# Neighbouring steps and the order of weight conversions in the first pair of an attention and two-FFN kernel

## The chip, the core and the metric

The program runs on one NeuronCore of a Trainium2 chip. Five engines have queues of their own, and each works through its queue in the order in which the program was written: TensorE (PE, with the weight loads shown apart as PEld), VectorE (DVE), ScalarE (ACT), GpSimd (POOL) and SyncE (SP), which here only issues DMAs. An instruction that has to wait for another engine holds up everything behind it in its own queue. The metric is the device time of one execution in microseconds; lower is better.

## What is computed

Attention over the feature axis, and two feed-forward networks one after the other, on 6016 tokens of width 256 with a hidden width of 2048:

```python
qn = q / (norm(q, axis=1) + 1e-06); kn = k / (norm(k, axis=1) + 1e-06)
a = softmax(kn.T @ qn / tau)              # 256 x 256
x = v @ a                                  # 6016 x 256
h = x @ w_in;  g = h * clip(h + 3, 0, 6) / 6;  x = g @ w_out     # first FFN
h = x @ w_in2; g = max(h, 0) ** 2;             out = g @ w_out2  # second FFN
```

The result has to be good to fp32. PE multiplies in the fast fp32r format, so every operand is kept as a high part and a rest, and each product is three matmuls: high x high, rest x high, high x rest. The high part is a cast on ACT (`nc.scalar.copy` in `split`, L124 of the profile), the rest is a subtraction on DVE or POOL (L126).

## The kernel before

The tokens are cut into six *pairs* of two blocks (n = 0 and 1, up to 512 tokens each). The attention matrix is folded into the first layer: v @ a @ w_in is computed as v @ (a @ w_in), so the first-layer weights of the first FFN are products too, called *m1* in the code, made in four quarters c4 (tiles `mp` in PSUM, then `wa_<c4>h` and `wa_<c4>l`, and `a` for a part of them). From the second pair on, eight products are done as seven by Strassen's scheme, and all work stands in a list of events with a place each (`at`, `extra`, `run`).

The first pair is different, and it is what the change touches. Its weights are not ready when it begins. It runs 32 *steps*; step a is one block n and one slice f of 128 hidden features (from step 4 on a = 2f + n). In a step, in the words used below:

- **h(a)**, the first product on PE (`product`, `whole_product`; six matmuls at L311, the first ones at L321 to L323), into one of four PSUM banks taken in turn;
- **relu(a)** on ACT (L651; tile `r`) and **gate(a)** on DVE (L653; tile `g`), which reads the PSUM bank and `r` and frees the bank;
- **hi(a)** on ACT and **lo(a)** on DVE, the high part and the rest of g (tile `gs`, four buffers);
- **s(a)**, the second product on PE (`second_both`; six matmuls at L676, four that use hi(a), then two that use lo(a)), accumulated in `acc`.

`drain(LAG)` with LAG = 2 puts s(a-2) into step a, behind h(a+1).

Into the same queues go the conversions of the weights of the first FFN from float64 words, fourteen in this list: `wi1` (an eighth of w_in) and `wo1` (an eighth of w_out). A conversion has five stages: 0 `magnitude` (ACT, L155), 1 `sign` (ACT L158 and DVE L159), 2 `high` (DVE L162), 3 `low` (DVE L167), 4 the split (ACT L124, DVE L126). `START` gives each one its place: `issue()` is called twice in a step and each call does what the plan has for the next place. The last stage also calls `feed()`, which issues the DMA of a later unit on SP, into one of three staging slots. For the first five conversions (DENSE) the stages have five places in a row, for the others the places 0, 3, 4, 5 and 6 from the start.

A quarter of m1 is made in steps 5, 13 and 21 (`m1_whole`, two products into two PSUM banks), and taken out of PSUM one step later (`m1_out`: three casts on ACT at L493 and three rests on DVE at L495; `m1_keep`: two copies at L503). The first h that uses it is h(8), h(16) or h(24). POOL makes the sums and rests of the quarters 0 and 1 that the Strassen pairs need (`m`, L216, and the rests `wa_0l`, `wa_1l` at L126), and the operands of the second pair, at places of the event list that `run` reaches at the end of each step.

Of the kernel before, what the change touches and what calls it, by code (L numbers as in the profile page):

```python
# [12 lines left out]
AF = mybir.ActivationFunctionType  # L13
ALU = mybir.AluOpType
# [7 lines left out]
KC = C // P  # L22
# [8 lines left out]
LAG = 2  # L31
# [5 lines left out]
EARLY_AT = {15: (0, 1), 16: (2,), 18: (3, 4)}  # L37


START = [-5, -3, 0, 3, 6] + [9 + 4 * k for k in range(9)]  # L40
DENSE = 5
SIGN = -(2 ** 31)
APART = 2.6
# [13 lines left out]
def attention_then_two_ffns(  # L57
# [30 lines left out]
    nc = tc.nc  # L88
# [25 lines left out]
    three = const.tile([P, 1], F32, name="three")  # L114
# [6 lines left out]
    def split(hi, lo, x, part=2, eng=nc.vector):  # L121

        if part != 1:
            nc.scalar.copy(hi, x)  # L124
        if part != 0:
            eng.tensor_tensor(out=lo, in0=x, in1=f32(hi), op=ALU.subtract)  # L126
# [46 lines left out]
    wi1, wo1 = {}, {}  # L173
# [151 lines left out]
    with tc.manual_schedule():  # L325
# [10 lines left out]
        for gi, n in enumerate(GROUPS):  # L336
            src = wpool.tile([P, 1024], F32, tag=f"wo{gi % NU}", name=f"qk{gi}")[:, :2 * n * C]
            nc.sync.dma_start(
                out=src.rearrange("p (t x c) -> p t x c", t=n, x=2), in_=qk[:, t:t + n, :, :]
# [5 lines left out]
            if gi == TAU_AT:  # L345
# [4 lines left out]
                    out=tq[:, 2:4], in0=tq[:, 2:4], scalar1=tau_sb, scalar2=1.0, op0=ALU.mult, op1=ALU.mult  # L350
# [11 lines left out]
        et = [hpool.tile([P, KC, C], F32R, tag="o", bufs=4, name=f"et{s}") for s in ("h", "l")]  # L362

        order = [
            ("wo1", 0), ("wi1", 2), ("wo1", 1), ("wi1", 3), ("wo1", 2), ("wi1", 4), ("wo1", 3), ("wi1", 5),
            ("wo1", 4), ("wi1", 6), ("wo1", 5), ("wi1", 7), ("wo1", 6), ("wo1", 7),
        ]
        loaded = []

# [100 lines left out]
        def m1_whole(c4, i):  # L470
            mps[c4, i] = bank([P, 512], f"mp{c4}_{i}")
            low_last(mps[c4, i], [
                ([t[:, j, :] for t in wi1[c4]], [t[:, i, j * P:(j + 1) * P] for t in et]) for j in range(KC)
            ], False)
# [138 lines left out]
        def tmp(tag, w, name, **kw):  # L613
            return hpool.tile([P, WMAX], F32, tag=tag, name=name, **kw)[:, :w]

        def g_tile(w, name):
            t = gpool.tile([P, 2, WMAX], F32R, tag="g", name=name)[:, :, :w]
            return [t[:, i, :] for i in range(2)]


        w0 = WIDTHS[0]
        steps = [(n, f) for f in range(KF) for n in range(2)]
        steps[:4] = [(0, 0), (0, 1), (1, 0), (1, 1)]
        hs = {}
        pending = []
# [8 lines left out]
        def product(at, k):  # L634
            if at < len(steps):
                n, f = steps[at]
                if k == 0:
                    hs[at] = bank([P, WMAX], f"h0_{n}_{f}")[:, :w0]
                passes(hs[at], [(weight0(f, k), x0[k, n])], k == 0, k == KC - 1)

        def whole_product(at):
            if at < len(steps):
                n, f = steps[at]
                hs[at] = bank([P, WMAX], f"h0_{n}_{f}")[:, :w0]
                low_last(hs[at], [(weight0(f, k), x0[k, n]) for k in range(KC)])

        def first(at_step, between):
            n, f = steps[at_step]
            h = hs.pop(at_step)
            r = tmp("r", w0, f"r0_{n}_{f}")  # L650
            nc.scalar.activation(r, h, AF.Relu, bias=three)  # L651
            g = tmp("g32", w0, f"g0_{n}_{f}")
            nc.vector.scalar_tensor_tensor(out=g, in0=r, scalar=6.0, in1=h, op0=ALU.min, op1=ALU.mult)  # L653
            between()
            gs = g_tile(w0, f"gs0_{n}_{f}")
            if at_step == len(steps) - 1:
                at(1.6, lambda: split(*gs, g, 0))
                at(3.0, lambda: split(*gs, g, 1))
            else:
                split(*gs, g)  # L660
            return gs

        def second(n, f, gs):
            return [
# [16 lines left out]
        def drain(limit):  # L681
            while len(pending) > limit:
                second_both(*pending.pop(0))


        plan = {}
        for k, at in enumerate(START):
            for st, after in enumerate(range(5) if k < DENSE else (0, 3, 4, 5, 6)):
# [4 lines left out]
        def issue():  # L693
            for k, st in sorted(plan.get(place[0], ())):
                loaded[k][st]()
                if st == 4:
                    feed()
            place[0] += 1
# [4 lines left out]
        def at(place, go):  # L703
            events.append((place, len(events), go))
# [158 lines left out]
        k = 0  # L863
# [67 lines left out]
        for kk in range(KC):  # L931
            for a in range(2):
                product(a, kk)
        for a, (n, f) in enumerate(steps):
            gs = first(a, issue)
            pending.append((n, f, gs))

            part, since = divmod(a + M1_LEAD, 8)
            if 0 < part < 4 and since == 1:
                for i in range(KC):  # L940
                    m1_out(part, i)
                m1_keep(part)
            late_products = (a + 1) % 8 == 0 and a < 24
            if late_products:
                drain(LAG)
            if a:
                whole_product(a + 1)
            if 0 < part < 4 and since == 0:
                for i in range(KC):
                    m1_whole(part, i)  # L950
            drain(LAG)
            issue()

            run(-(len(steps) - 1 - a) * SLOTS / 4)


        for x, go in zip(LEFT_AT, [(n, f, d, gs) for n, f, gs in pending for d in range(KC)], strict=True):
            n, f, d, gs = go
# [48 lines left out]
```

## Time and profile before

| what | value |
|---|---|
| median of 3 runs | 1042.24 us (1042.06 to 1043.7) |
| the profiled execution's own time | 1042.34 us |
| its span, first to last instruction | 1040.6 us |
| PE busy | 1031.6 us, 99% of the span |
| DVE busy | 852.5 us, 82% |
| ACT busy | 665.0 us, 64% |
| POOL busy | 28.9 us, 3% |
| PE clock granted | 1.00 of full speed (2.4 GHz) |
| share of the chain that ended last | PE 90%, DVE 3%, ACT 3%, DMA 2% |

A matmul's duration in the profile is longer than its distance to the next, since matmuls overlap; a PE that loses time can therefore look busy. What it loses is seen from the distance of its starts, or where the profile writes an idle time in brackets. In the timeline a line is a start in microseconds from the span's start, a duration in microseconds, engine, line, operation, written tile and read tiles, shapes, and the number of instructions merged into it; in brackets stands idle time just before it, and what ended it.

### The profile page before, as it was taken

How to read it: one execution, taken by the hardware profiler on the slowest of the kernel's cores; microseconds unless marked ns; L12 is line 12 of the kernel's file. 1: busy time of each engine (PE TensorE's matmuls, PEld its weight loads, DVE VectorE, ACT ScalarE, POOL GpSimd, SP SyncE). 2: the span in 40 equal slices, each digit the busy share in tenths (PEclk: the TensorE clock that was granted, in tenths of full speed). 3: DMA queues.
4: the chain of work that ended last, by engine and by line, in shares of the span. 5: the costliest groups of instructions: out<-in, count | busy, mean ns of one | idle time of the engine just before them, and what ended most of it. 6: DMA issues, size and time to landing. Idle time of an engine off the chain costs nothing.

```text
span 1040.6 us, 12968 instructions
## 1 busy us (share of the span) xinstructions
PE 1031.6 (99%) x4630; PEld 866.4 (83%) x4630; DVE 852.5 (82%) x1429; ACT 665.0 (64%) x1200; POOL 28.9 (3%) x33
## 2 busy tenths in 40 slices
PE   9999999999999999999999999999999999999998
PEld 8878788888888888888998888888888888888997
DVE  7898868889989889988988688688688688778765
ACT  6787777787788778877876445445445455445443
POOL 0012240000000000000000000000000000000000
PEclk9999999999999999999999999999999999999999
DMA  9911204003403403212755002002001100200100
GB/s 368 349 41 43 79 3 140 1 1 117 157 1 116 157 1 117 97 56 96 254 197 187 1 1 81 1 1 80 2 1 45 37 1 3 74 1 1 41 1 36
DMA packets 25936, 77.64 MB, mean 75 GB/s; under 512 B 2832, under 2 KB 4880, under 8 KB 25872
## 3 DMA queue, kind: packets, MB, share of 16 engines
q1 hardware_dynamic: 25872, 76.82, 20.9%
q8 instruction: 36, 0.59, 0.2%
q14 instruction: 28, 0.23, 0.1%
HBM read 52.95 MB, written 23.86 MB: 74 GB/s over the span
## 4 chain that ended last, share of the span: by engine, by line
PE 90%; DVE 3%; ACT 3%; DMA 2%; issue 1%; POOL 0%; ACTq 0%; SPq 0%; POOLq 0%
PE acc L323 15%; PE acc L321 15%; PE acc L322 15%; PE y L322 8%; PE y L321 8%; PE y L323 8%; PE q L321 4%; PE q L322 4%; PE q L323 4%; PE acc L676 2%; PE h L311 2%; PE x L321 2%; PE x L323 2%; PE x L322 2%; DMA qk<-in_qk 2%
## 5 line engine op out<-in xcount | busy, mean ns | idle before, releaser
L126 DVE TENSOR_TENSOR gs<-g,gs 128x512 fp32r<-128x512 f32 (+1 forms) x384 | 260.7, 679 | 59.8 <-ACT gs L828 47.8
L323 PE MATMUL acc<-gs,wo 128*128 128x512 f32 (+1 forms) x708 | 272.5, 385 | 0.1
L322 PE MATMUL acc<-gs,wo 128*128 128x512 f32 (+1 forms) x708 | 272.5, 385 | 0.0
L321 PE MATMUL acc<-gs,wo 128*128 128x512 f32 (+1 forms) x708 | 272.4, 385 | 0.0
L828 ACT CAST gs<-g 128x512 fp32r<-128x512 f32 (+1 forms) x352 | 208.1, 613 | 27.7 <-DVE g L819 19.0
L323 PEld LDWEIGHTS acc<-gs,wo 128*128 128x128 f32 x708 | 132.9, 188 | 25.3 <-DVE gs L126 0.5
L321 PEld LDWEIGHTS acc<-gs,wo 128*128 128x128 f32 x708 | 132.9, 188 | 24.4
L322 PEld LDWEIGHTS acc<-gs,wo 128*128 128x128 f32 x708 | 132.9, 188 | 24.3
L801 ACT COPY se<-y 128x512 f32<-128x512 f32 (+1 forms) x88 | 50.8, 577 | 124.0 <-PE y L323 123.9
L805 DVE TENSOR_TENSOR h<-q,se 128x512 f32<-128x512 f32 (+1 forms) x88 | 59.6, 678 | 65.6 <-ACT se L801 65.1
L801 ACT COPY su<-y 128x512 f32<-128x512 f32 (+1 forms) x88 | 50.9, 578 | 87.0 <-PE y L323 76.1
L824 DVE SCALAR_TENSOR_TENSOR g<-h 128x512 f32<-128x512 f32 (+1 forms) x144 | 97.0, 674 | 0.0
L811 ACT ACTIVATE r<-h,three 128x512 f32<-128x512 f32 (+1 forms) x120 | 85.5, 713 | 7.9 <-DVE h L805 7.7
L819 DVE SCALAR_TENSOR_TENSOR g<-r,h 128x512 f32<-128x512 f32 (+1 forms) x120 | 80.9, 674 | 3.9 <-ACT r L811 3.8
L813 ACT ACTIVATE r<-y 128x512 f32<-128x512 f32 (+1 forms) x48 | 28.3, 589 | 62.3 <-PE y L323 62.3
L805 DVE TENSOR_TENSOR h<-q,su 128x512 f32<-128x512 f32 (+1 forms) x88 | 59.5, 676 | 1.6
L805 DVE TENSOR_TENSOR h<-x,sa 128x512 f32<-128x512 f32 (+1 forms) x88 | 59.2, 673 | 0.0
L801 ACT COPY sa<-y 128x512 f32<-128x512 f32 (+1 forms) x88 | 50.8, 577 | 6.6 <-PE y L323 0.4
L824 DVE SCALAR_TENSOR_TENSOR g<-y,r 128x512 f32<-128x512 f32 (+1 forms) x48 | 32.7, 681 | 23.2 <-ACT r L813 22.7
L676 PE MATMUL acc<-gs,wo 128*128 128x512 f32 x180 | 45.5, 391 | 1.0 <-ACT gs L124 1.0
L300 PE MATMUL s<-qk 128*128 128x256 f32 x188 | 42.0, 385 | 0.0
L676 PEld LDWEIGHTS acc<-gs,wo 128*128 128x128 f32 x180 | 33.5, 188 | 9.1 <-ACT gs L124 2.2
(247 smaller groups left out, 1801.1 us busy)
## 6 DMA issues: line engine op xcount, KB each, us to landing
qk<-in_qk SPq DMA_DIRECT2D x23, 512.0 KB, 7.4
wo<-in_w_out SPq DMA_DIRECT2D x16, 512.0 KB, 5.1
wi<-in_w_in SPq DMA_DIRECT2D x10, 512.0 KB, 4.6
x2d<-o SPq DMA_DIRECT2D x20, 256.0 KB, 2.4
raw<-x2d SPq DMA_DIRECT2D x10, 512.0 KB, 5.8
out<-o SPq DMA_DIRECT2D x20, 256.0 KB, 2.2
raw<-in_vt SPq DMA_DIRECT2D x8, 512.0 KB, 5.9
wo2d<-wo2s SPq DMA_DIRECT2D x8, 512.0 KB, 2.9
```

What stands on the lines that cost most here:

```text
L126: eng.tensor_tensor(out=lo, in0=x, in1=f32(hi), op=ALU.subtract)
L300: nc.tensor.matmul(s_ps[i], lhsT=x[:, C + i * P:C + (i + 1) * P], rhs=x[:, :C], start=(t == 0), stop=(t == NT - 1))
L321: nc.tensor.matmul(ps, lhsT=ah, rhs=bh, start=first, stop=False, skip_group_check=more)
L322: nc.tensor.matmul(ps, lhsT=al, rhs=bh, start=False, stop=False, skip_group_check=more)
L323: nc.tensor.matmul(ps, lhsT=ah, rhs=bl, start=False, stop=last, skip_group_check=more)
L676: nc.tensor.matmul(acc[0, 0, n, d], lhsT=wo1[u][:, i, at + d * P:at + (d + 1) * P], rhs=gs[k], start=f == 0 and (i, k) == (0, 0), stop=f = ...
L801: nc.scalar.copy(s[tag], s["y"])
L805: nc.vector.tensor_tensor(out=s[which], in0=s[ps], in1=s[tag], op=ALU.add)
L811: nc.scalar.activation(s["r" + which], h, AF.Relu, bias=three)
L819: nc.vector.scalar_tensor_tensor(out=g, in0=s["r" + which], scalar=6.0, in1=h, op0=ALU.min, op1=ALU.mult)
L824: nc.vector.scalar_tensor_tensor(out=g, in0=h, scalar=0.0, in1=r, op0=ALU.max, op1=ALU.mult)
L828: nc.scalar.copy(gs[which][0], s["g" + which])
```

## The change

Two things are changed, both in the first pair. The function `first` is split into `relu0`, `gate0` and `part0`, and the loop calls them for different steps: in step a stand the relu of step a+1, the gate and the high part of step a, and the rest of step a-1. In the steps 7, 15 and 23 (`late_products`) s(a-2) goes ahead of h(a+1) as before, and relu(a+1) behind hi(a). Of the two m1 products the second goes behind the second product of the step. And in the table of conversions wi1 5 goes ahead of wo1 3, wi1 7 ahead of wo1 5, and all from the fifth on start at other places (the fifth at 10 where it was 6, the last at 46 where it was 41).

```diff
-START = [-5, -3, 0, 3, 6] + [9 + 4 * k for k in range(9)]
+START = [-5, -3, 0, 3, 10, 13, 17, 20, 25, 29, 33, 36, 41, 46]
...
-            ("wo1", 0), ("wi1", 2), ("wo1", 1), ("wi1", 3), ("wo1", 2), ("wi1", 4), ("wo1", 3), ("wi1", 5),
+            ("wo1", 0), ("wi1", 2), ("wo1", 1), ("wi1", 3), ("wo1", 2), ("wi1", 4), ("wi1", 5), ("wo1", 3),
...
-        def first(at_step, between):
...
-            nc.scalar.activation(r, h, AF.Relu, bias=three)
...
-            between()
-            gs = g_tile(w0, f"gs0_{n}_{f}")
...
-                split(*gs, g)
+        def relu0(at_step):
...
+                nc.scalar.activation(rs[at_step], hs[at_step], AF.Relu, bias=three)
+
+        def gate0(at_step):
...
+        def part0(at_step, part):
+            if at_step >= 0:
+                (hi, lo), g = gs0.pop(at_step) if part else gs0[at_step]
+                split(hi, lo, g, part)
...
+        relu0(0)
         for a, (n, f) in enumerate(steps):
-            gs = first(a, issue)
-            pending.append((n, f, gs))
-
             part, since = divmod(a + M1_LEAD, 8)
+            late_products = (a + 1) % 8 == 0 and a < 24
+            if late_products:
+                drain(LAG - 1)
+            if a:
+                whole_product(a + 1)
+            if not late_products:
+                relu0(a + 1)
+            pending.append((n, f, gate0(a)))
+            issue()
...
+                part0(a, 0)
+            if late_products:
+                relu0(a + 1)
+            part0(a - 1, 1)
             if 0 < part < 4 and since == 1:
                 for i in range(KC):
                     m1_out(part, i)
                 m1_keep(part)
-            late_products = (a + 1) % 8 == 0 and a < 24
-            if late_products:
-                drain(LAG)
-            if a:
-                whole_product(a + 1)
-            if 0 < part < 4 and since == 0:
-                for i in range(KC):
-                    m1_whole(part, i)
+            m1 = 0 < part < 4 and since == 0
+            if m1:
+                m1_whole(part, 0)
             drain(LAG)
+            if m1:
+                m1_whole(part, 1)
             issue()
```

What this does to the queues is shown at three places. The first is DVE at the start of the pair. In the names `g_0_0` is the g of block 0, slice 0 (step 0), `g_0_1` that of step 1, `gs_0_0` the rest of step 0; `tawi_2`, `tawo_1` are weights in conversion. Before:

```order
L653 SCALAR_TENSOR_TENSOR g_0_0_588<-r_0_0_586,h_0_0_572 128x512
L167 ISA tawi_2_536<-tawi_2_536,tywi_2_538 128x1024
L126 TENSOR_TENSOR gs_0_0_595<-g_0_0_588,gs_0_0_595 128x512
L126 TENSOR_TENSOR wi1l_599<-tawi_2_536,wi1h_598 128x512
L159 TENSOR_SCALAR tawo_1_591<-wo_1_432 128x512
L653 SCALAR_TENSOR_TENSOR g_0_1_608<-r_0_1_606,h_0_1_576 128x512
L162 SCALAR_TENSOR_TENSOR tawo_1_591<-tbwo_1_592,tawo_1_591 128x512
L126 TENSOR_TENSOR gs_0_1_611<-g_0_1_608,gs_0_1_611 128x512
```

and after the change, on the same engine and from the same instruction on:

```order
L658 SCALAR_TENSOR_TENSOR g_0_0_590<-r_0_0_586,h_0_0_572 128x512
L167 ISA tawi_2_536<-tawi_2_536,tywi_2_538 128x1024
L126 TENSOR_TENSOR wi1l_600<-tawi_2_536,wi1h_599 128x512
L159 TENSOR_SCALAR tawo_1_594<-wo_1_432 128x512
L658 SCALAR_TENSOR_TENSOR g_0_1_616<-r_0_1_588,h_0_1_576 128x512
L162 SCALAR_TENSOR_TENSOR tawo_1_594<-tbwo_1_595,tawo_1_594 128x512
L126 TENSOR_TENSOR gs_0_0_592<-g_0_0_590,gs_0_0_592 128x512
```

The rest of step 0, `gs_0_0`, which stood second behind its gate, now stands sixth, behind the gate of step 1.

The second place is ACT in step 6, where the first-layer weights `wa_1h` of quarter 1 are taken out of PSUM. The steps 5, 6 and 7 are `1_2`, `0_3` and `1_3` here. Before:

```order
L124 CAST gs_1_2_722<-g_1_2_716 128x512
L651 ACTIVATE r_0_3_754<-h_0_3_725,three 128x512
L158 ACTIVATE tywi_4_712<-raw13h 128x512
L124 CAST gs_0_3_760<-g_0_3_756 128x512
L493 ACTIVATE wa_1h<-mp_0_732,rs_504 128x2x128
```

and after:

```order
L124 CAST gs_1_2_713<-g_1_2_711 128x512
L158 ACTIVATE tywo_2_716<-wo_2_603 128x512
L653 ACTIVATE r_1_3_751<-h_1_3_744,three 128x512
L124 CAST gs_0_3_755<-g_0_3_753 128x512
L493 ACTIVATE wa_1h<-mp_0_720,rs_504 128x2x128
```

Ahead of the weights now stands the relu of step 7, `r_1_3`, where that of step 6 stood.

The third place is DVE around steps 9 (`1_4`), 10 (`0_5`) and 11 (`1_5`). Before:

```order
L653 SCALAR_TENSOR_TENSOR g_0_5_881<-r_0_5_879,h_0_5_859 128x512
L159 TENSOR_SCALAR tawi_5_845<-raw13l 128x512
L126 TENSOR_TENSOR gs_0_5_885<-g_0_5_881,gs_0_5_885 128x512
L162 SCALAR_TENSOR_TENSOR tawi_5_845<-tbwi_5_846,tawi_5_845 128x512
L653 SCALAR_TENSOR_TENSOR g_1_5_909<-r_1_5_907,h_1_5_888 128x512
L167 ISA tawi_5_845<-tawi_5_845,tywi_5_847 128x1024
L126 TENSOR_TENSOR gs_1_5_912<-g_1_5_909,gs_1_5_912 128x512
```

and after:

```order
L658 SCALAR_TENSOR_TENSOR g_0_5_876<-r_0_5_845,h_0_5_838 128x512
L159 TENSOR_SCALAR tawi_5_832<-raw13l 128x512
L126 TENSOR_TENSOR gs_1_4_849<-g_1_4_847,gs_1_4_849 128x512
L162 SCALAR_TENSOR_TENSOR tawi_5_832<-tbwi_5_833,tawi_5_832 128x512
L658 SCALAR_TENSOR_TENSOR g_1_5_904<-r_1_5_874,h_1_5_867 128x512
L167 ISA tawi_5_832<-tawi_5_832,tywi_5_834 128x1024
L126 TENSOR_TENSOR gs_0_5_878<-g_0_5_876,gs_0_5_878 128x512
```

The kinds of instruction and the conversion among them are the same; the two rests belong to one step earlier each.

## Rows read from the trace of the kernel before

**Rows 1.** Chain of waits, last steps of the first pair: start, us, what.
```profile
139.16 1.36 PE acc L676 x6
```

**Rows 2.** Timeline of PE, first pair: start us, us, what, idle before.
```profile
58.59 1.07 PE L311 MATMUL h<-x,wa_0h 128*128 128x512 f32 x4
...
61.31 1.52 PE L676 MATMUL acc<-gs,wo 128*128 128x512 f32 x6
...
72.20 0.50 PE L311 MATMUL mp<-wi1h,eth 128*128 128x512 f32 x1 [0.63 <-DVE g L653]
...
79.14 1.07 PE L311 MATMUL h<-x,wa_1h 128*128 128x512 f32 x4
...
119.16 1.65 PE L676 MATMUL acc<-gs,wo 128*128 128x512 f32 x6 [0.96 <-ACT gs L124]
...
152.59 0.39 PE L321 MATMUL y<-x,wa_0h 128*128 128x512 f32 x1
```

**Rows 3.** Waits from 50 to 157 us: us in total, times, longest.
```profile
DVE gs L126 <- ACT gs L124: 8.9, 16, 1.3
DVE g L653 <- ACT r L651: 8.1, 11, 1.3
```

**Rows 4.** Timeline of DVE, steps 0 and 1.
```profile
59.50 1.18 DVE L167 CUSTOM_DVE_ANT_0 tawi<-tawi,tywi 128x1024 uint16<-128x1024 uint16 x1
60.60 1.23 DVE L126 TENSOR_TENSOR gs<-g,gs 128x512 fp32r<-128x512 f32 x1
61.76 0.68 DVE L126 TENSOR_TENSOR wi1l<-tawi,wi1h 128x512 fp32r<-128x512 f32 x1
62.36 0.41 DVE L159 TENSOR_SCALAR tawo<-wo 128x512 int32<-128x512 int32 x1
62.69 0.67 DVE L653 SCALAR_TENSOR_TENSOR g<-r,h 128x512 f32<-128x512 f32 x1
63.29 0.68 DVE L162 SCALAR_TENSOR_TENSOR tawo<-tbwo,tawo 128x512 int32<-128x512 int32 x1
```

**Rows 5.** Timeline of ACT, step 0.
```profile
60.71 0.62 ACT L124 CAST wi1h<-tawi 128x512 fp32r<-128x512 f32 x1 [0.48 <-DVE tawi L167]
```

**Rows 6.** Timeline of ACT, around the m1 casts of step 6.
```profile
75.29 0.68 ACT L651 ACTIVATE r<-h,three 128x512 f32<-128x512 f32 x1
...
77.27 0.47 ACT L493 ACTIVATE wa_1h<-mp,rs 128x256 fp32r<-128x256 f32 x1
...
78.00 0.69 ACT L493 ACTIVATE wa_1h<-mp,rs 128x512 fp32r<-128x512 f32 x1
```

**Rows 7.** Timeline of POOL.
```profile
89.78 1.29 POOL L126 TENSOR_TENSOR wa_0l<-m,wa_0h 128x512 fp32r<-128x512 f32 x1 [1.80 <-ACT wa_0h L124]
...
92.04 1.07 POOL L216 TENSOR_TENSOR m<-m,m 128x256 f32<-128x256 f32 x1
...
94.22 1.24 POOL L216 TENSOR_TENSOR m<-m,m 128x256 f32<-128x256 f32 x1
...
112.30 2.58 POOL L126 TENSOR_TENSOR wa_1l<-m,wa_1h 128x512 fp32r<-128x512 f32 x2 [16.84 <-ACT wa_1h L124]
```

**Rows 8.** Timeline of DVE beside POOL's work from 89.78 on.
```profile
90.92 0.43 DVE L159 TENSOR_SCALAR tawi<-raw13l 128x512 int32<-128x512 int32 x1
91.70 0.81 DVE L126 TENSOR_TENSOR gs<-g,gs 128x512 fp32r<-128x512 f32 x1 [0.34 <-ACT gs L124]
92.43 1.23 DVE L162 SCALAR_TENSOR_TENSOR tawi<-tbwi,tawi 128x512 int32<-128x512 int32 x1
93.58 0.67 DVE L653 SCALAR_TENSOR_TENSOR g<-r,h 128x512 f32<-128x512 f32 x1
94.18 0.68 DVE L167 CUSTOM_DVE_ANT_0 tawi<-tawi,tywi 128x1024 uint16<-128x1024 uint16 x1
94.94 1.06 DVE L126 TENSOR_TENSOR gs<-g,gs 128x512 fp32r<-128x512 f32 x1
```

**Rows 9.** Timeline of DVE beside POOL's wa_1l.
```profile
113.97 1.46 DVE L167 CUSTOM_DVE_ANT_0 tawo<-tawo,tywo 128x1024 uint16<-128x1024 uint16 x1
```

More of the change, by code (lines that the diff above doesn't have):

```diff
@@ L364, in attention_then_two_ffns @@
         order = [
[L365 to L366 removed]
+            ("wo1", 0), ("wi1", 2), ("wo1", 1), ("wi1", 3), ("wo1", 2), ("wi1", 4), ("wi1", 5), ("wo1", 3),
+            ("wo1", 4), ("wi1", 6), ("wi1", 7), ("wo1", 5), ("wo1", 6), ("wo1", 7),
         ]
@@ L645, in whole_product @@
                 low_last(hs[at], [(weight0(f, k), x0[k, n]) for k in range(KC)])
-        def first(at_step, between):
+        rs, gs0 = {}, {}
+        def relu0(at_step):
+            if at_step < len(steps):
+                n, f = steps[at_step]
+                rs[at_step] = tmp("r", w0, f"r0_{n}_{f}")
+                nc.scalar.activation(rs[at_step], hs[at_step], AF.Relu, bias=three)
+        def gate0(at_step):
             n, f = steps[at_step]
-            h = hs.pop(at_step)
-            r = tmp("r", w0, f"r0_{n}_{f}")
-            nc.scalar.activation(r, h, AF.Relu, bias=three)
             g = tmp("g32", w0, f"g0_{n}_{f}")
-            nc.vector.scalar_tensor_tensor(out=g, in0=r, scalar=6.0, in1=h, op0=ALU.min, op1=ALU.mult)
-            between()
-            gs = g_tile(w0, f"gs0_{n}_{f}")
[L656 to L659, printed above, removed]
-                split(*gs, g)
-            return gs
+            nc.vector.scalar_tensor_tensor(
+                out=g, in0=rs.pop(at_step), scalar=6.0, in1=hs.pop(at_step), op0=ALU.min, op1=ALU.mult
+            )
+            gs0[at_step] = g_tile(w0, f"gs0_{n}_{f}"), g
+            return gs0[at_step][0]
+        def part0(at_step, part):
+            if at_step >= 0:
+                (hi, lo), g = gs0.pop(at_step) if part else gs0[at_step]
+                split(hi, lo, g, part)
         def second(n, f, gs):
@@ L933, in attention_then_two_ffns @@
                 product(a, kk)
+        relu0(0)
         for a, (n, f) in enumerate(steps):
-            gs = first(a, issue)
-            pending.append((n, f, gs))
             part, since = divmod(a + M1_LEAD, 8)
+            late_products = (a + 1) % 8 == 0 and a < 24
[7 more added lines that the diff above has]
+            issue()
+            if a == len(steps) - 1:
+                at(1.6, lambda: part0(len(steps) - 1, 0))
+                at(3.0, lambda: part0(len(steps) - 1, 1))
+            else:
+                part0(a, 0)
+            if late_products:
+                relu0(a + 1)
+            part0(a - 1, 1)
             if 0 < part < 4 and since == 1:
```

## Prediction

> **What bounds the kernel now.** I read the page first, then the chain of waits, then TensorE's (PE's) timeline of the first pair, then the other queues around its gaps. In the chain a block of six matmuls takes 1.36 us [rows 1], so one takes 0.2267 us while nothing holds PE. The change touches only the first pair, where PE runs its steps from 58.59 to 152.59 us [rows 2]. In between stand 396 matmuls: 30 products of 6, three pairs of m1 products (36), 30 second products of 6. They need 396 x 0.2267 = 89.77 us; the stretch takes 94.00. So 4.2 us are lost there, which is all that this change can win. Two of the gaps are seen directly [rows 2]: the second m1 product at 72.20 waited for its PSUM bank, which a gate of VectorE (DVE) still read, and the second product at 119.16 waited for a high part. After 152.59 PE is fed without gaps until the last evictions.
>
> I call h(a) the product of step a, relu(a) and hi(a) ScalarE's (ACT's) two instructions for it, gate(a) and lo(a) DVE's two, s(a) the second product, which uses hi(a) in its first four matmuls and lo(a) in its last two.
>
> **The change part by part.** No instruction is added or removed. Three things move: relu(a+1) goes ahead of gate(a) and hi(a); lo(a) goes from step a to step a+1, behind gate(a+1); the conversions start later and in another order. The sum is made against the profiled execution's 1042.34 us (1040.6 span and 1.7 around it), 0.1 us over the median of the runs, 1042.24.
>
> *Waits inside a step.* DVE loses 8.1 us waiting for a relu and 8.9 for a high part in this stretch [rows 3]. Both waits nearly go: relu(a) is a step old when gate(a) comes, hi(a) is done when lo(a) comes. That is worth something to PE only where DVE was late; it buys back the 4.2 us at most. What is late next is lo itself: it now has one step (12 matmuls, 2.72 us) less until s(a) needs it.
>
> *The first step: 2.0 us lost.* s(0) starts at 61.31 [rows 2], so its lo matmuls are due at 61.31 + 4 x 0.2267 = 62.22. Before, lo(0) stands at 60.60 and ends at 61.83 [rows 4], in time. After, DVE's queue from the L167 of the weights at 59.50 on is: rest of the weights, L159, gate(1), L162, lo(0). The L167 ends at 60.68, the cast of the weights on ACT runs from 60.71 to 61.33 as before [rows 4, 5], and the rest can start at 61.35 instead of 61.76. From there the starts follow at the distances of rows 4: L159 0.60 later (61.95), gate(1) 0.33 later (62.28), L162 0.60 later (62.88), lo(0) 0.60 later (63.48), and with the 0.68 of an undisturbed rest [rows 4] it ends at 64.16. PE waits 64.2 - 62.2 = 2.0 us. The same count one step on puts lo(1) at 67.1, with its matmuls due at 66.9: 0.2 more. From lo(2) on the rest is in time, since s(0)'s wait has moved all of PE back. Its bound from below would be 0, if DVE took the rows in another order; from above 2.5, with 0.1 for each restart.
>
> *The m1 bank and the high parts: those gaps go.* In step 5 the second m1 product now stands behind s(3), and gate(4), whose bank it takes, is done at 70.8 by the same count, before PE wants it. The other old gaps go with the old order, so of the 4.2 none is counted in the new kernel.
>
> *New first weights: 0, with 0.3 for each of three from above.* In step 6 relu(7) now stands on ACT ahead of hi(6) and of the three casts that make the first-layer weights of the next quarter. It waits for h(7). With 84 matmuls from 58.59 and the 2.2 us above, h(8), the first user of those weights, starts at 77.63 + 2.2 = 79.83 (before: 79.14 [rows 2]). h(7) ends three blocks earlier, at 77.2 with its tail; relu 0.68, a cast 0.62, two of 0.37 and one of 0.69 [rows 5, 6] end at 79.96. The first of them is there by 79.0, the last is due two matmuls into h(8), at 80.28. So it is just hidden. If that cover goes, PE waits at h(8), h(16) and h(24). What it does cost is DVE: lo(5) ends about 74.8 and the rests of these weights stand ahead of all else until ACT delivers, near 78.9: four idle microseconds, after which DVE's backlog has to be worked off at some 2.3 us of work per 2.72 us step (gate and lo 1.2, half a conversion of 0.33 + 3 x 0.60).
>
> *Steps 9 and 10: 1.2 us lost.* GpSimd (POOL) works from 89.78 to 95.46 [rows 7], and DVE's instructions with both operands in SBUF that begin inside a POOL instruction end only some 0.55 us after it: the L162 at 92.43 takes 1.23 us and ends at 93.66, POOL's ended at 93.11. The gate at 93.58, which reads PSUM, takes its 0.67 [rows 7, 8]. From 80.5, where the last rest of the new weights leaves DVE, thirteen instructions (12 x 0.60 + 0.33 = 7.5 us) and 1.7 us of waits (0.6 for casts, 1.1 behind POOL's first wa_0l) lead to the L159 at 89.8. From an L159 to the end of the second lo behind it DVE took 90.92 to 96.00 before [rows 8], 5.1 us. After, the same kinds begin 0.6 us before POOL's second wa_0l is through, so lo(9) ends at 89.8 + 0.6 + 1.6 = 92.0 and lo(10) at 89.8 + 0.6 + 5.1 = 95.5. Counting 60 matmuls from h(8), s(9)'s lo is due at 91.6 and s(10)'s at 94.3. PE waits 0.4, then 95.5 - 94.7 = 0.8. Before, the second lo of that row was lo(11), needed much later. Bounds: 0, if POOL misses these instructions (six of them undisturbed take 3.3 us: lo(10) at 93.1), and 1.9.
>
> The Trainium skill ("SBUF — State Buffer", section "Who interferes with whom") says that a VectorE instruction with two SBUF inputs fully blocks against a GpSimd instruction that reads SBUF, and one with a single SBUF input does not. By that rule every lo and every L162 and L167 can be held and no gate, which leaves both of these terms as they stand; a reader who took the two as sharing bandwidth would put them near 0 and get 1041.0. The rows agree with the rule.
>
> *Step 18: 1.7 us lost.* The same with wa_1l: POOL's two run 2.58 us without a gap [rows 7], and the L167 that met them took 1.46 [rows 9]. After, the two casts that release them stand two instructions behind hi(16) on ACT, while DVE comes to L162, gate(17), L167 and lo(16). Walking both queues on from h(16) with the same distances, POOL starts 1.95 us before lo(16) is due; the L167 is held by the first, lo(16) by the second, and lo(16) ends 2.58 + 0.55 + 0.55 = 3.7 us after POOL's start: 1.7 late. Bounds 0 and 1.8.
>
> *Start table and DMAs: 0.* Each weight is still finished before its first use (wo_3, now behind two wi units, ends a step ahead of s(12)). The second pair's load now stands on SP behind wo_6, which waits for a staging slot, some 5 us later than before; POOL's two sums from it fall into steps 21 and 22, where DVE is waiting anyway, and the second pair starts ten steps later. If that cover goes, up to 0.8 is lost at 152.59. It goes into the upper end.
>
> *Sum.* New gaps 2.2 + 1.2 + 1.7 + 0.7 for restarts and the third quarter = 5.8, against 4.2 before: +1.6, so **1043.9 us**. With all bounds low 2.6 - 4.2 = -1.6 (1040.7), with all high 2.5 + 0.9 + 1.9 + 1.8 + 0.8 = 7.9, +3.7 (1046.0).
>
> **The rivals.**
> *The port collisions miss.* ACT's casts set when POOL runs, and half a microsecond of drift is enough. Then only the start and the restarts remain, 2.6 us: 1040.7. For it: the old kernel met the same POOL work and lost little. Against it: the two meetings are set by neighbouring rows, not by chance.
> *Faster for good.* The freed 17 us of DVE waits are real at the start too: DVE reaches lo(0) by 62.2, the new order loses under 1 us in all: 1042.3 - 3.4 = 1038.9. It decides whether the L159, gate(1) and L162 delay lo(0). Against it: the four stand in front of it in the queue.
> *Slower: relu(a+1) blocks ACT.* At each of the three m1 steps relu waits for a product behind 18 other matmuls while the casts that need nothing stand behind it. If DVE's backlog then reaches PE again after each, at 1 us each beside the collisions, the sum is +3.5: 1045.8. It decides from the point where the casts end after 80.3. Against it: the count above ends at 79.96.
>
> **How the numbers follow.** About 0.2% (2.1 us: 1040.2 to 1044.3) is what a measurement can tell here. Forecast 0.50, own range 1042.6 to 1045.2, of which 0.29 lies under 1044.3 and 0.21 over it. Collisions miss 0.20, nearly all within 0.2%. Faster 0.15. Slower 0.15. So faster 0.17, same 0.47, slower 0.36. The range 1039.8 to 1045.8 leaves out most of the faster case and the top of the slower.
>
> **What would show it.** A gap on PE of about 2 us at s(0), put down to DVE's gs; none before the second m1 product of step 5; DVE idle for some 4 us ahead of the wa_1l rests; PE held by gs of DVE near 92 to 96 and near 115; h(8) near 79.8 and the second pair's first product near 154. The forecast is wrong if s(0) runs through, or if PE loses under 3 us between 58.6 and that product.

## The result, and the profile after

The changed kernel takes 1050.05 us (median of 6 runs, 1048.49 to 1051.74), the kernel before beside it 1042.15 us. The ratio is 1.0074, 95% interval 1.0063 to 1.0084: slower by 7.9 us. 1043.9 had been forecast, with 1045.8 as the upper end. The profiled execution took 1048.49 us with a span of 1046.7 us, 6.1 us over the span before. The 1.5 us between it and the median are taken up under the clock below. The forecast misses the median by 6.1 us: 5.0 are lost in the stretch shown next beyond the 5.8 that were forecast, 1.5 are these, and 0.5 come back because the stretch began earlier.

All of it is in the first pair. This is the timeline of PE in that stretch, columns as in [rows 2]:

```profile
58.12 1.07 PE L311 MATMUL h<-x,wa_0h 128*128 128x512 f32 x4
...
60.84 1.07 PE L682 MATMUL acc<-gs,wo 128*128 128x512 f32 x4
63.80 0.73 PE L682 MATMUL acc<-gs,wo 128*128 128x512 f32 x2 [1.89 <-DVE gs L126]
...
79.59 1.07 PE L311 MATMUL h<-x,wa_1h 128*128 128x512 f32 x4
...
83.81 0.73 PE L682 MATMUL acc<-gs,wo 128*128 128x512 f32 x2 [0.33 <-DVE gs L126]
...
95.74 0.73 PE L682 MATMUL acc<-gs,wo 128*128 128x512 f32 x2 [0.47 <-DVE gs L126]
...
105.84 1.39 PE L311 MATMUL h<-x,wa_2h 128*128 128x512 f32 x4
107.07 0.92 PE L311 MATMUL h<-x,wa_2l 128*128 128x512 f32 x2
...
117.11 0.74 PE L682 MATMUL acc<-gs,wo 128*128 128x512 f32 x2 [1.38 <-DVE gs L126]
...
120.85 0.73 PE L682 MATMUL acc<-gs,wo 128*128 128x512 f32 x2 [0.69 <-DVE gs L126]
...
138.83 0.74 PE L682 MATMUL acc<-gs,wo 128*128 128x512 f32 x2 [0.71 <-DVE gs L126]
...
148.56 0.74 PE L682 MATMUL acc<-gs,wo 128*128 128x512 f32 x2 [1.24 <-DVE gs L126]
...
158.71 0.39 PE L321 MATMUL y<-x,wa_0h 128*128 128x512 f32 x1
```

From 58.12 to 158.71 are 100.59 us, where [rows 2] gave 94.00. The matmuls need 89.77, so 10.8 us are lost, against 4.2 before: +6.6. The stretch began 0.47 us earlier, and +6.6 - 0.47 is the 6.1 us of the span. Each gap that is put down to gs is a second product whose last two matmuls wait for lo. The true loss is the distance of the starts less 0.2267 us per matmul, with 0.12 us more behind each for the restart: at s(0), 63.80 - 60.84 - 4 x 0.2267 = 2.05.

The waits of the same stretch as in [rows 3], 50 to 157 us (us in total, times, longest):

```profile
ACT r L653 <- PE h L311: 15.0, 10, 3.2
...
PE acc L682 <- DVE gs L126: 6.7, 7, 1.9
DVE wa_1l L495 <- ACT a L493: 4.5, 1, 4.5
DVE g L658 <- ACT r L653: 4.0, 4, 1.4
DVE wa_3l L495 <- ACT a L493: 3.4, 1, 3.4
DVE wa_2l L495 <- ACT a L493: 3.2, 1, 3.2
```

The change did what it says: DVE's 8.9 us of waiting for a high part are gone, and its 8.1 us for a relu are 4.0. In their place DVE waits 11.1 us in three pieces ahead of the m1 rests, ACT waits 15 us for h, and PE waits seven times for a rest. Before, PE waited for none.

At the start DVE stands as the prediction counted it [rows 4]:

```profile
59.03 1.20 DVE L167 CUSTOM_DVE_ANT_0 tawi<-tawi,tywi 128x1024 uint16<-128x1024 uint16 x1
60.92 0.69 DVE L126 TENSOR_TENSOR wi1l<-tawi,wi1h 128x512 fp32r<-128x512 f32 x1 [0.69 <-ACT wi1h L124]
61.53 0.42 DVE L159 TENSOR_SCALAR tawo<-wo 128x512 int32<-128x512 int32 x1
61.86 0.68 DVE L658 SCALAR_TENSOR_TENSOR g<-r,h 128x512 f32<-128x512 f32 x1
62.46 0.68 DVE L162 SCALAR_TENSOR_TENSOR tawo<-tbwo,tawo 128x512 int32<-128x512 int32 x1
63.06 0.68 DVE L126 TENSOR_TENSOR gs<-g,gs 128x512 fp32r<-128x512 f32 x1
```

lo(0) is the last of these and ends at 63.74; PE goes on at 63.80. In step 6, ACT and behind it DVE [rows 6]:

```profile
77.13 0.69 ACT L653 ACTIVATE r<-h,three 128x512 f32<-128x512 f32 x1 [3.10 <-PE h L311]
...
78.95 0.70 ACT L493 ACTIVATE wa_1h<-mp,rs 128x512 fp32r<-128x512 f32 x1
```

```profile
79.10 0.48 DVE L495 SCALAR_TENSOR_TENSOR wa_1l<-mp,rs,wa_1h 128x256 fp32r<-128x256 f32 x1 [4.52 <-ACT a L493]
...
105.90 0.48 DVE L495 SCALAR_TENSOR_TENSOR wa_2l<-mp,rs,wa_2h 128x256 fp32r<-128x256 f32 x1 [3.23 <-ACT a L493]
...
133.74 0.48 DVE L495 SCALAR_TENSOR_TENSOR wa_3l<-mp,rs,wa_3h 128x256 fp32r<-128x256 f32 x1 [3.38 <-ACT a L493]
```

ACT stands 3.10 us at a relu whose product PE has not made; the casts wait behind it though their input is there. DVE waits 4.52 us for the casts, with its rests and gates queued behind. It is the same at quarters 2 and 3.

Where POOL works, DVE's instructions with two SBUF operands stretch; this is called a collision below. POOL first [rows 7], then DVE [rows 8, 9]:

```profile
113.53 2.98 POOL L126 TENSOR_TENSOR wa_1l<-m,wa_1h 128x512 fp32r<-128x512 f32 x2 [18.39 <-ACT wa_1h L124]
117.50 1.31 POOL L758 TENSOR_TENSOR t<-raw 128x512 f32<-128x512 f32 x1 [0.99 <-DMA raw<-in_vt]
118.89 1.36 POOL L758 TENSOR_TENSOR t<-raw,t 128x512 f32<-128x512 f32 x1
136.59 1.64 POOL L765 TENSOR_TENSOR x<-raw,x 128x512 fp32r<-128x512 f32 x1 [16.34 <-ACT x L761]
...
146.23 1.73 POOL L758 TENSOR_TENSOR raw<-raw,t 128x512 f32<-128x512 f32 x1
```

```profile
94.46 1.22 DVE L126 TENSOR_TENSOR gs<-g,gs 128x512 fp32r<-128x512 f32 x1
...
113.76 1.61 DVE L167 CUSTOM_DVE_ANT_0 tawi<-tawi,tywi 128x1024 uint16<-128x1024 uint16 x1
115.30 1.76 DVE L126 TENSOR_TENSOR gs<-g,gs 128x512 fp32r<-128x512 f32 x1
...
118.18 0.92 DVE L159 TENSOR_SCALAR tawi<-wi 128x512 int32<-128x512 int32 x1
119.02 1.78 DVE L126 TENSOR_TENSOR gs<-g,gs 128x512 fp32r<-128x512 f32 x1
...
136.99 1.78 DVE L126 TENSOR_TENSOR gs<-g,gs 128x512 fp32r<-128x512 f32 x1
...
145.03 1.80 DVE L126 TENSOR_TENSOR wo<-tawo,wo 128x512 fp32r<-128x512 f32 x1 [0.56 <-ACT wo L124]
146.75 1.76 DVE L126 TENSOR_TENSOR gs<-g,gs 128x512 fp32r<-128x512 f32 x1
```

Each of PE's gaps from s(16) on that is put down to gs has its stretched gs: the one from 119.02 ends at 120.80, and PE goes on at 120.85; the one from 136.99 ends at 138.77, and PE at 138.83. The two POOL sums from 117.50 on came from the second pair's load, which landed then. L159, which has one SBUF operand, is held as well: 0.92 us here where it took 0.42 at 61.53.

### The profile page after: what moved, and what is told of

It is laid out like the page before. It is cut to its first block, busy times and chain, and to the rows that moved or that the text cites. A ratio compares the mean times of both kernels' runs of the same rounds, so it can differ in the third digit from the quotient of the medians.

```text
span 1046.7 us, 12978 instructions
## 1 busy us (share of the span) xinstructions
PE 1032.5 (99%) x4630; PEld 865.8 (83%) x4630; DVE 856.5 (82%) x1429; ACT 664.2 (63%) x1200; POOL 30.1 (3%) x33
## 4 chain that ended last, share of the span: by engine, by line
PE 92%; DVE 4%; ACT 2%; issue 1%; DMA 0%; SPq 0%; DVEq 0%; ACTq 0%
PE acc L323 15%; PE acc L322 15%; PE acc L321 15%; PE y L322 7%; PE y L321 7%; PE y L323 7%; PE q L321 4%; PE q L323 4%; PE q L322 4%; PE s L300 3%; PE x L323 2%; PE x L321 2%; PE x L322 2%; PE h L311 2%; PE acc L682 2%; DVE gs L126 1%
## 5 line engine op out<-in xcount | busy, mean ns | idle before, releaser
L126 DVE TENSOR_TENSOR gs<-g,gs 128x512 fp32r<-128x512 f32 (+1 forms) x384 | 264.8, 690 | 52.6 <-ACT gs L834 48.2
L321 PE MATMUL acc<-gs,wo 128*128 128x512 f32 (+1 forms) x708 | 272.4, 385 | 0.0
L321 PEld LDWEIGHTS acc<-gs,wo 128*128 128x128 f32 x708 | 132.9, 188 | 24.3
```

The costliest lines, as they stand in the source:

```text
L321: nc.tensor.matmul(ps, lhsT=ah, rhs=bh, start=first, stop=False, skip_group_check=more)
```

## The experiments

Fifteen kernels ran. The "stretch" is taken in the profiled execution, from the first h (L321) to the second pair's first y (L321); it starts 3.5 us before the rows above and has no part in the rest of the program, which took 888.0 us from that y on in most of them. The profiled executions of e4 and e15 contain the dip of the granted clock told at the end of this section, 1.6 and 1.4 us of their stretch; no other does. The medians of the changed kernel, e1, e4, e10 and e15 mix runs with the dip and runs without it. "PE for gs" is PE's waiting for a rest in the view of waits, 50 to 157 us.

| kernel | median us | ratio to before, 95% | stretch | PE for gs |
|---|---|---|---|---|
| before | 1042.15 to 1042.65 | | 97.52 | none |
| changed | 1050.05 | 1.0074 [1.0063, 1.0084] | 104.09 | 6.7 |
| e1 old table | 1049.67 | 1.0069 [1.0054, 1.0084] | 103.40 | 5.8 |
| e2 new table only | 1042.90 | 1.0000 [0.9990, 1.0009] | 97.50 | 1.0 |
| e3 rest back | 1041.01 | 0.9985 [0.9975, 0.9995] | 96.32 | none |
| e10 relu not ahead | 1044.92 | 1.0019 [1.0010, 1.0029] | 98.37 | 3.7 |
| e4 relu behind m1 | 1044.72 | 1.0015 [1.0004, 1.0027] | 100.03, 98.4 without the dip | 3.9 |
| e7 both back | 1041.54 | 0.9987 [0.9978, 0.9997] | 96.41 | 0.9 |
| e5 lag 3 | 1042.01 | 0.9998 [0.9988, 1.0007] | 96.64 | 0.5 |
| e14 rest back, lag 3 | 1042.48 | 0.9999 [0.9990, 1.0008] | 97.56 | none |
| e9 rest back, old table | 1042.16 | 0.9997 [0.9988, 1.0006] | 97.00 | none |
| e6 all POOL fills | 1043.13 | 1.0008 [0.9999, 1.0017] | 97.57 | 1.9 |
| e15 second pair's fills | 1047.13 | 1.0040 [1.0024, 1.0056] | 102.39, 101.0 without the dip | 4.0 |
| e16 m1 fills | 1045.82 | 1.0029 [1.0017, 1.0042] | 101.15 | 4.6 |
| e6b before, all POOL fills | 1039.02 | 0.9965 [0.9952, 0.9979] | 94.11 | none |
| e11 first rests back | 1048.99 | 1.0062 [1.0048, 1.0076] | 104.10 | 6.5 |
| e12 first gap filled | 1050.36 | 1.0074 [1.0061, 1.0088] | 104.95 | 4.9 |

The theories, in words: the table of conversions does it; the rest that comes a step later does it; the relu ahead of ACT's other work does it; and DVE held by POOL does it.

**The table.** e1 is the changed kernel with `START` and the order of before; e2 the kernel before with both new.

```diff
-START = [-5, -3, 0, 3, 10, 13, 17, 20, 25, 29, 33, 36, 41, 46]
+START = [-5, -3, 0, 3, 6] + [9 + 4 * k for k in range(9)]
```

> The new steps with the old START table and the old order of conversions. Theory R (the rest lo(a) stands one step later, so each delay of VectorE reaches the second product): no real change, 1047 to 1051, PE waiting for gs of VectorE for about 2 us at s(0) again. Rival T (the table is the cause): back to about 1042. Rival A (relu(a+1) ahead of the m1 casts blocks ScalarE): as R, 1047 to 1051.

> The kernel before with the new START table and the new order of conversions only. Theory R: the table moves little, 1040.5 to 1043; the fifth conversion stands four places later, so the 0.9 us at the second m1 product of step 5 may go, and others may come. Rival T: 1048 or more.

e1 stays with the changed kernel, e2 with the one before, both as theory R had it. The table is not the cause.

**Rest and relu, a square of four.** e3 puts lo(a) back into step a; e10 puts relu(a) back into step a and leaves the rest late; e4 leaves both as changed but puts relu(a+1) behind the three m1 casts in steps 6, 14 and 22; e7 is e3 and e4 together.

```diff
-            part0(a - 1, 1)
+            if a < len(steps) - 1:
+                part0(a, 1)
```

```diff
-            if not late_products:
+            m1_taken = 0 < part < 4 and since == 1
+            if not late_products and not m1_taken:
                 relu0(a + 1)
...
                 m1_keep(part)
+                relu0(a + 1)
```

> The changed kernel with lo(a) back in step a, right behind hi(a) in the program; relu(a+1) stays ahead, the table stays new. Theory R: the 2 us at s(0) and most other waits for gs of VectorE go, 1040.5 to 1043. Rival A: VectorE still idles 3 to 4.5 us ahead of each m1 rest and works off its backlog, so at least half of the 8 us stays: 1046 or more. Rival T: stays near 1050.

> The changed kernel with relu(a) back in step a, ahead of gate(a); the rest lo(a) stays one step late, the m1 order and the table stay new. It holds the late rest without what blocks ScalarE. Theory R: the late rest alone does it, and VectorE again waits for the relu in each step, so 1048 to 1053. Rival A (relu ahead of the m1 casts idles VectorE, its backlog meets PE): most of the loss goes, 1042 to 1045.

> The changed kernel with relu(a+1) put behind the casts and copies of m1 in the three steps that take m1 out (6, 14, 22), nothing else. Theory R: the start is untouched and the rests stay late, so at most 3 us are won: 1046.5 to 1050, with the 2.6 us at s(0) and s(1) there. Rival A: 1042 to 1044.5, and the 3 to 4.5 us of VectorE's idle time ahead of the m1 rests shrink to under 1.5.

> The changed kernel with both put back: lo(a) in step a and relu(a+1) behind the m1 casts in steps 6, 14 and 22. Theory R: against the kernel with only the rest back (1041.0) up to 1 us more is won, at the gaps before the first use of new m1 weights: 1040.0 to 1041.0. Rival A: clearly more, under 1039.5. If neither: 1041 to 1042.5.

e3 comes out as theory R had it, e10 and e4 as rival A had it (e4 0.2 us above its range), and e7 in neither range. So neither reason alone holds. e3 keeps the new place of the second m1 product as well, so that is not the cause either. With the rest in its own step the relu's place is worth nothing that shows (1041.0 ahead, 1041.5 behind the casts). With the rest late it is worth 5.3 us (1050.0 and 1044.7), and without any relu ahead the late rest costs 2.0 us at most (1044.9 against e2's 1042.9, which has the same table but the m1 products in their old place). So 3.2 us in e4 and 9.0 in the changed kernel are what a late rest costs over the same kernel with the rest back; the difference of 5.9 us is the two together. Part of the single prices is the clock: in the runs at a mean clock of 0.999 or more the medians are 1048.6 for the changed kernel and 1043.1 for e4, so that a late rest costs 7.6 and 1.6 us, and the two together still 6.1; e10's stretch, profiled without a dip, is 0.9 us longer than e2's. The waits of PE say the same, here in e10 and then in e4:

```profile
PE acc L682 <- DVE gs L126: 3.7, 4, 2.1
```

```profile
PE acc L682 <- DVE gs L126: 3.9, 4, 1.8
```

Four waits are left of seven, 2.1 and 1.8 of it at s(0). e3 has no such row, and is the fastest of all versions that compute everything: 1.4 us under the kernel before, its interval clear of 1.

**Slack instead of order.** e5 leaves the rest where the change put it and lets the second product come three steps behind the first.

```diff
-LAG = 2
+LAG = 3
```

> The changed kernel with LAG = 3: s(a) is taken out one step later (s(a-3) in step a), which gives each rest the 2.72 us back that the change took from it; the queues of VectorE and ScalarE stay as in the changed kernel. Theory R: 1040 to 1043, no wait at s(0), a few tenths at the first products with new m1 weights remain. Rival A: ScalarE is blocked as before and the gaps at h(8), h(16), h(24) (0.2, 0.6, 0.6) and the backlog behind them stay: 1045 or more. Rival T: 1048 or more.

```profile
PE acc L682 <- DVE gs L126: 0.5, 1, 0.5
```

8.0 us come back in the median and 7.45 in the stretch, and one wait of 0.5 us is left of 6.7, at s(0), where the theory had none; h(16) and h(24) still lose 0.64 and 0.63, as it had. The rest still comes late and is still held; what was missing is the step between it and its use. e14 adds the lag to e3, e9 gives e3 the old table.

> The changed kernel with every rest back in its own step and the second product three steps behind the first instead of two: both of the relations that bought time, so the version with the most room. If what PE still loses in the version with the rest back (about 0.45 in each of steps 2 to 5 and at step 24, 0.63 at the first new weights of h(16) and h(24)) hangs on the rest, two thirds go and it runs at 1039.5; if those are waits for the weights (m1 rests) and for PSUM banks, which a longer lag does not reach, it stays at 1041.0 +- 0.3.

> The version with the rest back in its own step (1041.0), with the old table and order of conversions. Asks where its 1.4 us under the kernel before come from. If from the new order of gate and relu alone, it stays at 1041.0 to 1041.3; if the new table shares in it, which by itself moved nothing (1042.9 against 1042.8 beside it), it goes to 1042 or more.

e14 misses both of its answers: with more lag e3 gets 1.5 us slower. PE waits there 0.8 us for an m1 bank that a gate holds and 0.5 us for weights, which it doesn't in e3; why the lag brings these is open. e9 comes out where the table was to share in e3's gain: its stretch is 0.7 us longer than e3's, its median 1.2 us higher. The two intervals overlap, so this is likely and not settled.

**DVE behind POOL.** e6 replaces POOL's sums and rests beside the first pair (of m1 and of the second pair's operands) by fills of the same tiles; these values are not computed. e15 does so for the second pair's operands only, e16 for m1 only, e6b for all of them in the kernel before. A fill waits for nothing and mostly runs earlier than the work it stands for (the m1 fills of quarter 1 at 74.64 in e6), so these kernels take POOL's work out of its place as well as its reads. In e15 the fills replace four sums and seven rests, more than its expectation names.

```diff
+        class Filler:
+            def tensor_tensor(self, out, in0, in1, op):
+                nc.gpsimd.memset(out.bitcast(F32) if out.dtype == F32R else out, 0.5)
...
-            return nc.gpsimd if first else nc.vector
+            return Filler() if first else nc.vector
```

> The changed kernel in which GpSimd's sums, rests and operands in and just behind the first pair are replaced by fills that read nothing, so their values are not computed. Theory P (most of the gaps behind step 2 are collisions of VectorE with GpSimd over SBUF): the waits at s(6), s(9), s(10), s(16), s(17), s(22), s(25) shrink to under 1 us in all, the 2.6 us at s(0) and s(1) and the 1.4 us at the new weights stay: 1043 to 1045. If collisions are not the cause, 1048 to 1051.

> The changed kernel with GpSimd's two sums and three rests of block 0 of the second pair (from 117 us on) replaced by fills of the same tiles, which read nothing; those values are not computed. Its m1 sums and rests stay. Prices the term that the prediction put at 0 (second pair's operands). Theory (DVE's instructions are held behind them, and that is what PE loses at s(17), s(22) and s(25), 0.98 + 1.00 + 1.52 = 3.5 us): 3 us less than the changed kernel, 1047 (1046.5 in the runs without a dip of the clock is 1045.2). Rival (the backlog behind the m1 rests does it, and whichever instructions DVE meets): under 1 us less, 1049 or more.

> The changed kernel with only GpSimd's sums and rests of the m1 quarters 0 and 1 (86 to 95 us and 113 to 116 us) replaced by fills; those values are not computed. Its operands of the second pair stay. Theory (each collision costs at its own place): s(6), s(9), s(10) and s(16) lose 0.6 + 0.4 + 0.75 + 1.7 = 3.4 us less, and the rest of the loss, at s(17), s(22) and s(25), stays: 1046.6. Rival (one backlog through the whole pair): the later places are relieved too, and it comes near the 1043.1 that all fills together gave.

> The kernel before with all the same work of GpSimd replaced by fills (values not computed). Says how much of the 7 us that the fills gave the changed kernel they give anyway. Theory (the collisions cost PE only where the rest is late): within 0.7 us of the kernel before, 1042.0 to 1042.8. Rival (GpSimd's work costs any version much): 1 us faster or more, 1041.3 or less.

e6 comes out as its theory had it (1043.1, with 0.3 us left of the waits it names), and so does e15 (1047). e16 is 0.8 us under its theory and far from its rival, but none of its runs has the dip, which half of the changed kernel's have; its stretch is 2.9 us shorter, where 3.4 were expected, because s(6) keeps its 0.61. PE's wait falls from 6.7 to 4.0 in e15, to 4.6 in e16 and to 1.9 in e6: 2.7 and 2.1 alone, 4.8 together. The collisions add up place by place, and no backlog is carried from the m1 work in the middle to the end: in e15 the waits at s(17), s(22) and s(25) go, in e16 those at s(10) and s(16), while s(22) and s(25) keep their 1.00 and 1.52. Another 0.3 us of what e16 and e6 win lies at s(0): there the L167 at 59.03, 1.20 us beside POOL's m1 sums in the changed kernel, takes 0.69 in e6. But e6b misses its theory: the kernel before gains 3.3 us by the same fills. Over the stretch POOL's work costs it 97.52 - 94.11 = 3.4 us and the changed kernel 104.09 - 97.57 = 6.5. So of the +6.57 between the two, 3.1 are collisions that reach PE in addition, and 3.46 are there without any (97.57 - 94.11): in e6, s(0) loses 1.76 and s(6) 0.48 before their restarts, h(16) and h(24) 0.62 each.

What a collision costs is a question of slack, not of the collision. The rests on DVE from 50 to 157 us, grouped by line (count, busy us, mean ns, idle before), before, after, in e3 and in e6:

```profile
L126 DVE TENSOR_TENSOR gs<-g,gs 128x512 fp32r<-128x512 f32 x32 | 23.6, 739 | 9.9 <-ACT gs L124 8.9
```

```profile
L126 DVE TENSOR_TENSOR gs<-g,gs 128x512 fp32r<-128x512 f32 x30 | 26.4, 882 | 0.0
```

```profile
L126 DVE TENSOR_TENSOR gs<-g,gs 128x512 fp32r<-128x512 f32 x32 | 26.8, 836 | 11.5 <-ACT gs L124 10.8
```

```profile
L126 DVE TENSOR_TENSOR gs<-g,gs 128x512 fp32r<-128x512 f32 x32 | 21.9, 685 | 2.5 <-ACT gs L124 2.5
```

e3's rests take longer than before in all (26.8 us, with two of 1.77 at 111.93 and 115.67 as after the change), and PE waits for none of them. Each has a step, 2.72 us, more until it is due, and a collision of 1.1 us fits in. In e3 DVE idles 11.5 us before its rests, 10.8 of it for the high part, more than before the change; that costs PE nothing.

**The start, and the clock.** In e11 the rests of steps 0 and 1 stand in their own steps. In e12 small matmuls stand between the fourth and the fifth matmul of s(0); there were 28 of them, twice what the expectation says, so they took 3.3 us and outlasted the wait by 1.0.

```diff
-            part0(a - 1, 1)
+            if a < 2:
+                part0(a, 1)
+            elif a > 2:
+                part0(a - 1, 1)
```

```diff
+                if (n, f) == (0, 0) and len(part) == 1:
+                    keep_busy(14, "fill")
```

> The changed kernel with lo(0) and lo(1) put back into their own steps; all later rests stay one step late. Asks what the stall of PE at s(0) is worth, and whether the dip of the granted clock hangs on it. Theory (stall, then clock): the 2.0 us stall at s(0) and the 0.4 at s(1) go, DVE is as late as before from step 5 on, so 1050.0 - 2.4 = 1047.6 without any later relief, and no run stands under a mean clock of 0.999; with the dip's share (about 2 us in half of the runs) gone too, the median is near 1046.5. Rival (the dip comes from the later gaps): half of the runs still show 0.998 and the median stays at 1048 or more. Rival (a stall at the start only lends time to DVE, which it then lacks later): PE loses the 2 us at s(6), s(9) and s(10) instead, and the time stays within 0.7 us of 1050.

> The changed kernel with 14 small matmuls (128x128, into the bank that keeps PE busy elsewhere, not used by the result) between the fourth and the fifth matmul of s(0): they take about 14 x 0.11 = 1.5 us, so that PE works through most of the wait for lo(0) that stands there. The wait itself stays. Theory (the dip of the clock follows PE's idleness): time per run as in those runs of the changed kernel that show no dip, 1048.5 to 1048.7, with no run under a mean clock of 0.999, a median 1 to 1.5 us lower. Rival (the dip has another cause, as the matmuls of step 5 or chance): the clock is under 0.999 in about half of the runs, and the median is 1050 as before.

e11's stretch is as long as the changed kernel's (104.10 and 104.09): s(0) and s(1) run through, and s(2), whose rest is now the first late one, loses 1.60 us with 1.30 of it idle. In these two kernels the loss stands at the first late rest, wherever that is. So the theory that the 2.4 us go falls, and its rival holds in the stretch but not in the place (s(2), and not s(6) to s(10)) nor in the median. What the theory said of the clock came true: all 4 runs have a mean granted clock of 1.000, and the median is 1.1 us lower. e12 has the clock that its theory wanted and the time of its rival.

In e4's profiled execution a dip of the granted clock can be seen. Four windows of 2 us: length, then busy time of PE, PEld, DVE, ACT and POOL, the granted clock, DMA:

```profile
62.00:64.00 2.00, 0.75 (x4) 0.28 (x2) 2.00 (x5) 1.45 (x4) 0.00 (x0) 1.00 0.19 27
64.00:66.00 2.00, 1.42 (x6) 1.20 (x7) 1.91 (x4) 1.96 (x4) 0.00 (x0) 1.00 0.73 236
66.00:68.00 2.00, 2.00 (x7) 1.55 (x6) 2.00 (x5) 1.56 (x3) 0.00 (x0) 0.51 0.00 0
68.00:70.00 2.00, 2.00 (x8) 1.56 (x7) 1.91 (x5) 1.22 (x2) 0.00 (x0) 0.64 0.00 0
```

PE stood still for 1.83 us until 64.58, went on at the full 2.4 GHz, and from 66 on the granted clock is 0.51 and 0.64, so 1.2 GHz for most of 4 us. The twelve matmuls from 65.15 on take 4.33 us where 2.72 would do: 1.6 us lost. In e15's, PE went on at 64.07 after 1.88 us of idling, and the window from 64 to 66 is already at 0.59, the next at 0.56: 1.4 us lost. The five kernels whose profile shows a gap of 1.8 us or more at s(0) (changed, e1, e4, e10, e15) have 19 of 34 runs at a mean clock of 0.998 or lower, and the medians of these runs are 1.5 to 2.4 us above those of the other runs. The other eleven kernels have none in 90 runs, e6 and e16 with gaps of 1.6 us among them, and the kernel before 4 in 87, whose cause is open. Two of e10's runs took 1044.4 and 1045.2 us at a mean clock of 1.000, so the clock is not all of the spread. The dip accounts for the 1.5 us between the changed kernel's profiled execution, which has none, and its median. That the dip follows from PE's idleness fits all of this, but e12's four runs are few, and its time, with 1.0 us of filling too much, doesn't test it.

## Why the prediction was wrong

The stretch loses 10.8 us, 5.8 were forecast. By places, with the restart behind each gap in the measured number:

| place | forecast | measured |
|---|---|---|
| s(0), s(1) | 2.0 + 0.2 | 2.17 + 0.19 |
| h(8), s(6) | 0 | 0.08 + 0.61 |
| s(9), s(10) | 0.4 + 0.8 | 0.26 + 0.75 |
| h(16), h(24) | 0 | 0.63 + 0.63 |
| s(16) | 1.7 | 1.67 |
| s(17) | 0 | 0.98 |
| s(22), s(25) | in 0.7 with all restarts | 1.00 + 1.52 |

**What held.** The queue at the start, the meetings in steps 9, 10 and 18, the end of the bank gap in step 5, DVE's 4 us ahead of the wa_1l rests, and h(8) (forecast 79.8, here 79.59): 5.0 us of the 10.8, each within 0.2 us of its term. The 4.2 us of old gaps did go.

**The step that failed first: "third quarter and restarts 0.7".** Steps 17 to 25 cost 3.5 us. Two collisions were walked through and the rest was given a lump. The queues there are the same kind as in step 18: after a wait of DVE for the m1 casts, a rest without slack meets POOL. The seven restarts alone, 0.12 us each, are 0.8, more than the whole lump.

**The second: the second pair's load "some 5 us later", its sums "where DVE is waiting anyway".** The load landed at about 117.5, and POOL's first sum from it began 1.5 us later than before, not 5. Before, that sum stood at 116.00:

```profile
116.00 1.30 POOL L752 TENSOR_TENSOR t<-raw 128x512 f32<-128x512 f32 x1 [1.13 <-DMA raw<-in_vt]
```

The second sum met lo(17). And the three rests and two more sums that POOL makes for that pair from 136.59 to 147.96 had not been placed at all. e15 prices the term that stood at 0: 2.7 us of PE's waiting. This is the loss of the first point over again and not one more: the waits that go in e15 are those at s(17), s(22) and s(25).

**The third: new first weights, 0.** The count was made for h(8) and came out right there; it was taken over to h(16) and h(24), where the m1 rest starts at 105.90 and 133.74, when h has started already, and each costs 0.63. In e10 and e4, with the casts ahead of that relu, neither place shows it. The bound of 0.3 was too low.

**The rival with the relu was the right mechanism at too low a chance and price.** It was to decide "from the point where the casts end after 80.3". They ended at 79.65, the weights were there for h(8), and the price came all the same, through DVE's 11.1 us of waiting with the rests queued behind. The condition looked at the casts' next user and not at what stands behind them on DVE. e4 puts the price at 5.3 us, against 3 in the rival. s(6), which stood at 0, belongs here: POOL is not at work near it, its 0.61 stays in e6 and e16, and it is gone in e4 and e10. The rival's sum was also not that of its terms: 1.6 and three times 1 are +4.6 (1046.9), not +3.5.

**Collisions.** The rival that they miss had 0.20; they met everywhere. What the prediction did not ask is what each held rest has in hand. By the sum it was one step less for 32 rests, with thirteen DVE instructions that the timeline shows held by POOL after step 6; only two places were priced. And the prediction took an instruction with one SBUF operand to be safe from POOL; L159 was held all the same in the changed kernel (0.94 at 90.11, 0.92 at 118.18).

**The clock** was not in the forecast at all: kernels with a gap of PE of about 2 us at s(0), which had been predicted, show the dip and about 2 us more in half of their runs.

**Two smaller slips.** The lower end of the sum, 2.6, is not all bounds low: it keeps the start at its full price though the bound given there is 0. And h(7) ends two blocks before h(8), not three; the 77.2 is right for two.

## What to carry to other kernels

When an operation is moved to a neighbouring step, count the slack from its end to its use in steps and give back what the move takes (a longer lag, another buffer) before counting which waits it frees: here one step of lag was worth 8.0 us in the median (7.45 in the stretch), and the waits that the change freed 1.4 us at most (e3). An instruction that waits for a late product, put ahead of ones that need nothing in the same queue, is paid for where what stands behind it has no slack: 5.3 us here with the rests late, nothing that shows with them in time. A term that repeats must be walked through at each of its places; the lump for the places not walked through was the largest error.

## What the runs showed of the hardware

A rest of 0.68 us becomes 1.76 to 1.80 us when it begins with a long stretch of POOL's work on SBUF operands still ahead, and 1.20 to 1.22 with a shorter one; it ends 0.55 us after POOL's instruction (115.30 + 1.76 = 117.06, POOL at 116.51). In e6 the same tiles are only written by POOL, and the rests take 685 ns on the mean: none is held, and this rest runs its normal time inside a run of three fills:

```profile
112.38 1.47 POOL L509 MEMSET x<- 128x512 f32 x3 [34.79 <-ACT wa_1h L124]
```

```profile
112.66 0.69 DVE L126 TENSOR_TENSOR gs<-g,gs 128x512 fp32r<-128x512 f32 x1
```

The Trainium skill (SBUF — State Buffer, "Who interferes with whom") says that such a VectorE instruction meets GpSimd's reads and not its writes; these runs agree. It frees an instruction with one SBUF input only outside VectorE's 2-port modes, a condition that the prediction left out. L159, which has one, is held by POOL's sums, and in e15 by fills too, where it takes 1.41 us in place of 0.42:

```profile
119.87 1.41 DVE L159 TENSOR_SCALAR tawi<-wi 128x512 int32<-128x512 int32 x1
```

The granted clock fell to its lower level after a gap of PE: in e4 when PE had been back at work for about 1.5 us behind a gap of 1.83 us, in e15 after less than 0.5 us behind one of 1.88. It cost 1.6 and 1.4 us there. Of the runs of the five kernels with such a gap, 19 of 34 have a mean clock as low as these two (0.998) or lower; why only some do is open.
